# Pooled attention and a gated feed-forward layer: later key and value loads on another queue, key pooling at an earlier step

## The chip, the cores and the metric

The kernel runs on one core of a Trainium2 chip. The core has five engines that run their own instruction streams: PE (TensorE, matrix products into PSUM banks), DVE (VectorE, elementwise work), ACT (ScalarE, activations and copies), POOL (GpSimd) and SP (SyncE, which here only issues transfers). Transfers between the chip's memory (DRAM) and the core's on-chip memory are issued by an engine onto its queue and carried out by 16 DMA engines that all queues share. The metric is the device time of one execution, in microseconds (us), lower is better.

## What is computed

Attention over keys and values that are averaged in groups of 8, and then a feed-forward layer with a SiLU between its two products. Cut to its core:

```python
# q, k, v: (8 batches, 8 heads, 576 positions, 64); w_in: (512, 2048); w_out: (2048, 512)
k_p = k.reshape(B, H, Sp, 8, D).mean(axis=3)      # Sp = 72
v_p = v.reshape(B, H, Sp, 8, D).mean(axis=3)
scores = scale * np.matmul(q, k_p.transpose(0, 1, 3, 2))
attn = softmax(scores)
x = heads side by side of np.matmul(attn, v_p)    # (4608, 512)
h = x @ w_in
g = h * (1.0 / (1.0 + np.exp(-h)))
return g @ w_out                                  # (4608, 512)
```

## The kernel before

The 4608 tokens are worked through in nine blocks of 512, `t` = 0 to 8. Each block has two products. `up(t, ...)` multiplies by `w_in` and applies SiLU, giving `h_T`; `down(t, ...)` for block 0 and `down_quarters(t, ...)` for the others multiply by `w_out` and store the result. From block 1 on, the products save multiplications: a product is cut into quarters, sums of quarters are formed (on the left `x_sum` at L454 for the first product and `h_sum` at L614 for the second), and seven partial products, numbered 1 to 7, are made in place of eight.

`down_quarters` makes its seven partial products in the order 2, 5, 1, 4, 3, 7, 6, in 112 steps of one matmul each. They accumulate into three PSUM banks, `P` (2, 4, 7), `Q` (5, 3, 6) and `R` (1). Between them VectorE and ScalarE take intermediate results out of the banks: after partial product 3 a copy on VectorE takes `Q` out into `o_sb` (L681), after 7 an addition takes `P` out (L685), and after 6 an addition takes `Q` out again (L689). Partial product 6 accumulates onto `Q`, so its first matmul has to wait for the copy at L681.

The attention of batch `t + 1` runs inside block `t` as small pieces between the steps of the products. They are "fillers": pairs of a step number and a function, called by `spread` at that step, so that a filler's instructions stand on each engine's stream behind what was issued up to that step. The order of every engine's instructions is therefore written out by hand through these numbers; an instruction that waits holds up all that stand behind it on its engine.

The keys and values of batch 0 to 2 are loaded in another layout (`load_slots`). For batches 3 to 7 a tensor of one batch arrives in two halves: `load_one` loads the first four of each eight rows that are averaged (`PH` = 256 numbers for each of 72 groups and 8 heads) into the buffer `raw`, and `load_rest` (L182) loads the other four onto POOL's queue with an addition into the same place, so it waits until the first half has landed. `load_one` goes through `load_rows` (L173), which issues two transfers on SP's queue, of 64 and of 8 partitions. There is one buffer for the keys (`k_raw`) and one for the values (`v_raw`). The queries of the batch (`load_q`) go onto POOL's queue too.

SP's queue also carries the stores of `down_quarters`, 16 for a block (L566).

Pooling: `pool_k(b, 0)` adds halves of the loaded rows (L188), `pool_k(b, 1)` makes the last addition in two instructions into `kp` (L193), which `k_transpose` turns over in the next block. `pool_v` does the same for the values, at step 10 of the second product.

In block `t` from 1 to 5, with `a = t + 1`, the fillers are issued as follows: at step 0 of the first product the first half of the keys of batch `t + 2`; at step 1 its queries (in block 5 at step 48, as eight pieces); at step 2 the second half of the keys; in the second product at step 10 `pool_v` of batch `t + 1`, at step 11 the first half and at step 12 the second half of the values of batch `t + 2`; at step 100 both stages of `pool_k` of batch `t + 2`. Numerators of the attention (`xT`, L403) are filled in at steps 56, 97 and 101. The next block begins with the five `x_sum` instructions at step 0.

Of the kernel before, what the change touches and what calls it, by code (L numbers as in the profile page):

```python
# [36 lines left out]
def kernel(  # L37
# [9 lines left out]
    nc = tc.nc  # L47
# [3 lines left out]
    SP = S // POOL  # L51
# [107 lines left out]
    PH = POOL // 2 * D  # L159

    def raw_tile(tag, heads, full=False):
        raw = big.tile([128, H * PH], FP32, tag=tag, name="raw")
        if full:
            return raw
        return raw[:SP, : H * PH].rearrange("k (h e) -> k h e", h=heads)

    def source(b, name):
        return (k if name == "k" else v)[b].rearrange("h (sp p) d -> sp h (p d)", p=POOL)


    def load_rows(eng, out, in_):
        for r0, r1 in ((0, 64), (64, SP)):
            eng.dma_start(out=out[r0:r1], in_=in_[r0:r1])  # L173

    def load_one(b, name):
        st = batches.setdefault(b, {})
        raw = raw_tile(f"{name}_raw", H)
        load_rows(nc.sync, raw, source(b, name)[:, :, :PH])
        st[f"{name}_raw"] = raw

    def load_rest(b, name):
# [5 lines left out]
    def add_halves(raw):  # L187
        nc.vector.tensor_add(  # L188
            out=raw[:, :, : 2 * D], in0=raw[:, :, : 2 * D], in1=raw[:, :, 2 * D :]
        )  # L190

    def add_rest(dst, raw):
        nc.vector.tensor_add(  # L193
            out=dst,
            in0=raw[:, :, :D].rearrange("k h (c d) -> k h c d", c=2),
            in1=raw[:, :, D : 2 * D].rearrange("k h (c d) -> k h c d", c=2),
        )

    def pool_k(b, stage):
        st = batches[b]  # L200
        raw = st["k_raw"]
        if stage == 0:
            add_halves(raw)
            return
        for i in range(2):
            add_rest(
                kp[:SP, i].rearrange("k c s d -> k s c d"), raw[:, 4 * i : 4 * (i + 1)]
            )
# [7 lines left out]
    def k_transpose(b, parts=(0, 1)):  # L216
        st = batches[b]
        kT_ps = ps_tile([128, 2, 2, SP], FP32, "at", "kT_ps")
        for a in parts:
            for c in range(2):  # L220
                nc.tensor.matmul(
                    kT_ps[:, a, c, :],
                    lhsT=kp[:, a, c].rearrange("k s d -> k (s d)"),
                    rhs=ident[:, :SP], start=True, stop=True,
                )
        a0, a1 = parts[0], parts[-1] + 1
        nc.scalar.copy(kz[b % 2][:, a0:a1], kT_ps[:, a0:a1])
# [40 lines left out]
    def slot_sums(name, j, halves=False):  # L268
        raw = row_tiles[name][j]
        dst = rows5[name][:, SA:] if j else rows5[name][:, :SA]  # L270
        w = RE // 4 if halves else RE // 2
        while w > D:
            nc.vector.tensor_add(  # L273
                out=raw[..., :w], in0=raw[..., :w], in1=raw[..., w : 2 * w]
            )
            w //= 2
        nc.vector.tensor_add(out=dst, in0=raw[..., :D], in1=raw[..., D : 2 * D])
# [10 lines left out]
    def select_k(b, a):  # L288
        st = batches[b]
        if a == 0:  # L290
            st["kz_ps"] = ps_tile([128, 2, 2, SP], FP32, "at", "kz_ps")
        for c in range(2):
            for s in range(4):
                for i, r, sp, m in segments(4 * a + s):
                    nc.tensor.matmul(
                        st["kz_ps"][32 * s : 32 * (s + 1), a, c, sp : sp + m],
                        lhsT=k5[:, i, c * DH : (c + 1) * DH],
                        rhs=ident[:, r : r + m], start=True, stop=True,
                    )

    def copy_k(b, a, copy=nc.vector.tensor_copy):
        copy(out=kz[b % 2][:, a], in_=batches[b]["kz_ps"][:, a])

    def select_v(b, a, tag="at"):
        st = batches[b]
        if a == 0:
            st["v_ps"] = ps_tile([128, H, D], FP32, tag, "v_ps")
            st["vp"] = mid.tile([SP, H, D], BF16, tag="vp", name="vp")
        for h in range(4 * a, 4 * (a + 1)):
            segs = list(segments(h))  # L310
            for j, (i, r, sp, m) in enumerate(segs):
                x = SP + r - sp
                nc.tensor.matmul(
                    st["v_ps"][:, h, :], lhsT=shifts[:, x : x + 128], rhs=v5[:, i],
                    start=(j == 0), stop=(j == len(segs) - 1),
                )

    def copy_v(b, a, copy=nc.vector.tensor_copy):
        hs = slice(4 * a, 4 * (a + 1))
        copy(out=batches[b]["vp"][:, hs, :], in_=batches[b]["v_ps"][:SP, hs, :])  # L320
# [468 lines left out]
    for t in range(NT):  # L789
        a = t + 1  # L790
        f_up, f_down = [], []
# [40 lines left out]
        if a < B:  # L832
            q_at = [15, 16, 17, 8] if t > 1 else [24, 25, 26, 2] if t else [82, 84, 86, 88]
            if t == 0:
                for j in range(2):
                    f_up.append((44 + 8 * j, lambda j=j: slot_sums("k", j)))
                    f_up.append((72 + 8 * j, lambda j=j: select_k(1, j)))
                    f_up.append((72 + 8 * j, lambda j=j: copy_k(1, j)))
                    f_down.append((20 + 10 * j, lambda j=j: slot_sums("v", j)))
                    f_down.append((37 + 3 * j, lambda j=j: select_v(1, j, "at")))  # L840
                    f_down.append((37 + 3 * j, lambda j=j: copy_v(1, j)))
            elif t == 1:
                for j in range(2):
                    f_up.append((0, lambda j=j: slot_sums("k", j, halves=True)))
                    f_up.append((22, lambda j=j: select_k(2, j)))
                    f_up.append((23, lambda j=j: copy_k(2, j)))
                    f_down.append((8, lambda j=j: slot_sums("v", j, halves=True)))
                    f_down.append((40, lambda j=j: select_v(2, j, "at")))
                    f_down.append((41, lambda j=j: copy_v(2, j)))
            else:  # L850
                f_up.append((22, lambda: k_transpose(a)))
                f_down.append((10, lambda: pool_v(a)))
            for n in range(4):
                f_to = f_down if t and n == 3 else f_up
                f_to.append((q_at[n], lambda n=n: q_transpose(a, n % 2, n // 2)))
            if t == 0:
                f_down.append((0, lambda: load_half_2("k", 0)))
                f_down.append((0, lambda: load_q(2)))
                f_down.append((0, lambda: load_half_2("k", 1)))
                for half in range(2):  # L860
                    f_down.append((31, lambda half=half: load_half_2("v", half)))
                for y in range(2):
                    for n in U_W:
                        f_down.append((6, lambda y=y, n=n: unit_weight_sum(y, n)))
            elif a + 1 < B:
                for stage in range(2):
                    f_down.append((100, lambda stage=stage: pool_k(a + 1, stage)))
                f_up.append((0, lambda: load_one(a + 1, "k")))
                f_up.append((48 if a + 1 == B - 1 else 1, lambda: load_q(a + 1)))
                f_up.append((2, lambda: load_rest(a + 1, "k")))  # L870
                f_down.append((11, lambda: load_one(a + 1, "v")))
                f_down.append((12, lambda: load_rest(a + 1, "v")))
            f_down.append((0, attn_tables))

            if t:
                sc_at, den_at, nu_at = (1, 31, 75), (31, 56, 97), (56, 97, 101)
            else:
                sc_at, den_at, nu_at = (1, 16, 30), (16, 30, 44), (44, 55, 56)
            for n, sg in enumerate(visits):
                f_down.append((den_at[n], lambda sg=sg: denominators(a, sg)))  # L880
                f_down.append((sc_at[n], lambda sg=sg: scores(a, sg)))

            for n, sg in enumerate(visits):
                if n < 2 or not 0 < t < B - 2:
                    f_down.append((nu_at[n], lambda sg=sg: numerators(a, sg)))
                if n == 0 and 1 < t < B - 1:
                    f_down.append((nu_at[n], lambda: numerators(a - 1, visits[2])))
# [34 lines left out]
```

The softmax here doesn't subtract the row's maximum and nothing guards it: scores larger than these inputs give would overflow.

## Time and profile before

| what | value |
|---|---|
| runs of this kernel | median 286.65 us (285.92, 286.42, 286.87, 287.04) |
| the profiled execution | 286.42 us, span 284.5 us |
| queue of POOL (software_dynamic) | 20.86 MB, 45.0% of the 16 DMA engines' span |
| queue of SP (hardware_dynamic) | 15.48 MB, 22.9% |
| SP issues of first halves (L173) | 20, median 0.60 us each, 57.2 to 191.3 us |
| POOL issues of second halves (L182) | 10, 1.38 to 1.43 us each |
| L182, issue to landing | 8.4, median 8.9, at most 11.3 us |
| L188 on VectorE | 10, median 1.195 us |
| L193 on VectorE into `kp` | 10, median 0.418 us |

The span runs from the first to the last instruction of the profiled execution; its time has what lies around it too. A group of a profile's rows gives a line of the kernel, an engine, the operation with output and input, the number of instructions, the busy time and the idle time of the engine just before. "Landing" is the time from the issue of a transfer until its data is in place. In a timeline a row's idle time and what ended it stand in square brackets. The chain of waits is followed back from the last instruction to what released each step, and is printed in order of time.

### The profile page before, as it was taken

To read this page: it belongs to the slowest core of one execution; us is meant where nothing else is said; L and a number is where in the kernel's file an instruction comes from. 1 tells how busy PE (TensorE), PEld (TensorE's weight loads), DVE (VectorE), ACT (ScalarE), POOL (GpSimd) and SP (SyncE) were. 2 spreads that over 40 slices of the span, in tenths; PEclk is the share of its full clock that TensorE was granted. 3 is DMA by queue.
4 is the path that set the end of the run, shared out by engine and by line. 5 is a ranking of instruction groups with operands and counts; after the bars stand their busy time and mean duration, and the time that the engine had idled before them with its cause. 6 is when DMAs were issued, how large, how long until landed. Compare 5 with 4: busy or idle time off the path is not lost.

```text
span 284.5 us, 6941 instructions
## 1 busy us (share of the span) xinstructions
PE 277.8 (98%) x2793; PEld 194.2 (68%) x2793; DVE 225.2 (79%) x404; ACT 183.7 (65%) x359; POOL 52.1 (18%) x68
## 2 busy tenths in 40 slices
PE   8989999999999999999999999999999999999995
PEld 3338544556777777667888785687667767787684
DVE  4986837899789896979697959886998686836773
ACT  1678765667577866687668856794779567325700
POOL 8744317312030013001020101062100000000000
PEclk9999999999999999999999999999999999999999
DMA  7999999894949557964979386739970032005004
GB/s 212 277 267 227 216 311 163 213 193 88 153 76 200 135 98 117 180 174 65 129 130 225 61 142 121 180 51 159 146 138 0 2 97 53 2 9 140 1 4 147
DMA packets 35296, 37.70 MB, mean 133 GB/s; under 512 B 9952, under 2 KB 27616, under 8 KB 35264
## 3 DMA queue, kind: packets, MB, share of 16 engines
q0 software_dynamic: 21760, 20.86, 45.0%
q1 hardware_dynamic: 12928, 15.48, 22.9%
q10 hardware_dynamic: 576, 0.92, 0.9%
q8 instruction: 22, 0.36, 0.6%
q14 instruction: 10, 0.08, 0.1%
HBM read 36.70 MB, written 9.44 MB: 162 GB/s over the span
## 4 chain that ended last, share of the span: by engine, by line
PE 87%; DVE 5%; DMA 3%; issue 1%; ACT 1%; SPq 1%; DVEq 0%; POOLq 0%
PE hp_ps L546 24%; PE o_psP L654 15%; PE o_psQ L654 14%; PE u_psQ L487 7%; PE u_psP L487 7%; PE o_psR L654 5%; PE sc_ps L350 4%; PE o_ps L581 3%; PE u_psR L487 2%; PE nu_ps L394 2%; DMA q_bf<-in_q_dram 2%; PE den_ps L368 2%; DMA out_dram<-o_sb 1%; SPq L566 1%; DVE w_sum L632 1%
## 5 line engine op out<-in xcount | busy, mean ns | idle before, releaser
L546 PE MATMUL hp_ps<-xT,w_in_sb 128*128 128x512 bf16 (+3 forms) x412 | 82.6, 340 | 0.5 <-ACT h_T L552 0.4
L552 ACT ACTIVATE h_T<-hp_ps 128x512 bf16<-128x512 f32 (+2 forms) x95 | 51.3, 545 | 26.9 <-PE hp_ps L546 25.6
L654 PEld LDWEIGHTS <-h_sum 128*128 128x128 bf16 x640 | 60.6, 98 | 12.0 <-issue 1.3
L546 PEld LDWEIGHTS <-w_in_sb 128*128 128x128 bf16 x412 | 39.3, 98 | 25.0 <-issue 1.4
L614 DVE TENSOR_TENSOR h_sum<-h_T 128x1024 bf16<-128x1024 bf16 (+1 forms) x72 | 50.8, 743 | 6.9 <-ACT h_T L552 6.9
L358 ACT ACTIVATE es<-sc_ps 72x384 bf16<-72x384 f32 (+1 forms) x100 | 38.9, 468 | 9.8 <-PE sc_ps L350 9.7
L487 PEld LDWEIGHTS <-w_sum 128*128 128x128 bf16 x300 | 29.2, 98 | 9.2 <-DVE x_sum L454 1.6
L654 PEld LDWEIGHTS <-h_T 128*128 128x128 bf16 x256 | 24.1, 98 | 4.4 <-issue 0.9
L403 DVE TENSOR_TENSOR xT<-nu_ps,rec 128x384 bf16<-128x384 f32 (+1 forms) x50 | 24.0, 532 | 0.3
L377 ACT ACTIVATE lnd<-den_ps 128x384 f32<-128x384 f32 (+1 forms) x23 | 11.1, 483 | 19.8 <-PE den_ps L368 19.8
L153 DVE STREAM_TRANSPOSE qT<-q_bf 128x576 bf16<-128x576 bf16 x32 | 23.0, 754 | 0.0
L495 ACT ACTIVATE h_T<-c_sb 128x512 bf16<-128x512 f32 x30 | 18.1, 625 | 5.0 <-DVE c_sb L519 5.0
L182 POOL DMA_DIRECT2D raw<-in_k_dram x5 | 7.0, 1397 | 74.2 <-DVE h_sum L614 24.0
L273 DVE TENSOR_TENSOR raw<-raw 128x384 f32<-128x384 f32 (+3 forms) x20 | 12.3, 614 | 8.3 <-DMA raw<-in_v_dram 4.7
L654 PE MATMUL o_psP<-w_out_sb,h_sum 128*128 128x256 bf16 x128 | 17.6, 273 | 0.0
L654 PE MATMUL o_psQ<-w_sum,h_sum 128*128 128x256 bf16 x128 | 16.7, 273 | 0.0
L654 PE MATMUL o_psQ<-w_out_sb,h_sum 128*128 128x256 bf16 x128 | 16.6, 273 | 0.0
L654 PE MATMUL o_psQ<-w_sum,h_T 128*128 128x256 bf16 x128 | 16.5, 273 | 0.0
L654 PE MATMUL o_psP<-w_sum,h_T 128*128 128x256 bf16 x128 | 16.5, 273 | 0.0
L654 PE MATMUL o_psR<-w_sum,h_sum 128*128 128x256 bf16 x128 | 15.7, 273 | 0.0
L182 POOL DMA_DIRECT2D raw<-in_v_dram x5 | 6.9, 1390 | 47.4 <-DVE kp L193 11.6
L654 PE MATMUL o_psP<-w_sum,h_sum 128*128 128x256 bf16 x128 | 15.4, 272 | 0.0
(78 smaller groups left out, 417.6 us busy)
## 6 DMA issues: line engine op xcount, KB each, us to landing
out_dram<-o_sb SPq DMA_DIRECT2D x128, 64.0 KB, 3.2
q_bf<-in_q_dram POOLq DMA_DIRECT2D x6, 576.0 KB, 11.7
raw<-in_k_dram SPq DMA_DIRECT2D x6, 512.0 KB, 5.3
raw<-in_k_dram POOLq DMA_DIRECT2D x5, 576.0 KB, 9.9
raw<-in_v_dram POOLq DMA_DIRECT2D x5, 576.0 KB, 8.7
raw<-in_v_dram SPq DMA_DIRECT2D x5, 512.0 KB, 9.6
w_in_sb<-in_moe_w_in_dram POOLq DMA_DIRECT2D x8, 256.0 KB, 8.6
w_out_sb<-in_moe_w_out_dram POOLq DMA_DIRECT2D x4, 512.0 KB, 13.6
```

The lines of the kernel that those rows point to most:

```text
L153: nc.vector.transpose(out=st["qT"][:, a, f * QF : (f + 1) * QF].rearrange("r i c p -> r (i c p)"), in_=st["q_bf"][:, a, f * n : (f + 1) * n],)
L182: nc.gpsimd.dma_start(out=batches[b][f"{name}_raw"], in_=source(b, name)[:, :, PH:], accum_op=ALU.add,)
L273: nc.vector.tensor_add(out=raw[..., :w], in0=raw[..., :w], in1=raw[..., w : 2 * w])
L350: nc.tensor.matmul(sc[s][:, cs], lhsT=kz[b % 2][rows, g, c, :], rhs=st["qT"][rows, g, i0:i1, c, :], start=(c == 0), stop=(c == 1),)
L358: nc.scalar.activation(es[:, s, :], sc[s], func=AF.Exp, scale=score_scale)
L403: nc.vector.tensor_mul(out=xT[:, 2 * g0 + c : 2 * (g0 + ng - 1) + c + 1 : 2, cols], in0=nu[c][:, :w].rearrange("r (g n) -> r g n", g=ng), ...
L487: nc.tensor.matmul(ps[bank][:, u, :], lhsT=w[:, kk, 128 * u : 128 * (u + 1)], rhs=x[:, kk, :], start=first and u == 0 and kk == 0, stop=kk ...
L495: nc.scalar.activation(h_T[:, g : g + 2, j * NQ : (j + 1) * NQ], src, func=AF.Silu)
L546: nc.tensor.matmul(hp_ps[:, r0:r1], lhsT=w_in_sb[:, kk, g * 128 : (g + 1) * 128], rhs=xT[:, kk, x0 : x0 + r1 - r0], start=(kk == 0), stop= ...
L552: nc.scalar.activation(h_T[:, g, n0 : n0 + n], hp_ps[:, :n], func=AF.Silu)
L614: nc.vector.tensor_tensor(out=h_sum[n][:, ks, :], in0=quarter(*a, ks), in1=quarter(*b, ks), op=op)
L654: nc.tensor.matmul(ps[b][:, c, :], lhsT=left(n, kt, c), rhs=W_OUT[n][:, kt, :], start=b not in begun, stop=kt == k1 - 1, skip_group_check= ...
```

## The change

The first halves of keys and values of batches 3 to 7 are issued on POOL's queue, as one transfer of 72 partitions, in place of two on SP's. The two stages of `pool_k` are issued at steps 73 and 81 of the second product in place of both at step 100. The step numbers of the loads are unchanged. In POOL's stream this gives, for each block from 1 to 5: first half of keys, queries, second half of keys, first half of values, second half of values.

```diff
-    def load_rows(eng, out, in_):
-        for r0, r1 in ((0, 64), (64, SP)):
-            eng.dma_start(out=out[r0:r1], in_=in_[r0:r1])
-
     def load_one(b, name):
         st = batches.setdefault(b, {})
         raw = raw_tile(f"{name}_raw", H)
-        load_rows(nc.sync, raw, source(b, name)[:, :, :PH])
+        nc.gpsimd.dma_start(out=raw, in_=source(b, name)[:, :, :PH])
         st[f"{name}_raw"] = raw
...
             elif a + 1 < B:
                 for stage in range(2):
-                    f_down.append((100, lambda stage=stage: pool_k(a + 1, stage)))
+                    f_down.append((73 + 8 * stage, lambda stage=stage: pool_k(a + 1, stage)))
                 f_up.append((0, lambda: load_one(a + 1, "k")))
                 f_up.append((48 if a + 1 == B - 1 else 1, lambda: load_q(a + 1)))
                 f_up.append((2, lambda: load_rest(a + 1, "k")))
                 f_down.append((11, lambda: load_one(a + 1, "v")))
                 f_down.append((12, lambda: load_rest(a + 1, "v")))
```

## The prediction, made before the changed kernel was run

> **What bounds the kernel now.** The page comes first: who is busy.
>
> ```profile
> span 284.5 us, 6941 instructions
> PE 277.8 (98%) x2793; PEld 194.2 (68%) x2793; DVE 225.2 (79%) x404; ACT 183.7 (65%) x359; POOL 52.1 (18%) x68
> PEclk9999999999999999999999999999999999999999
> raw<-in_k_dram SPq DMA_DIRECT2D x6, 512.0 KB, 5.3
> raw<-in_k_dram POOLq DMA_DIRECT2D x5, 576.0 KB, 9.9
> raw<-in_v_dram POOLq DMA_DIRECT2D x5, 576.0 KB, 8.7
> ```
>
> TensorE is busy for 98% of the span at full clock, so the moves of this change can only win back the few gaps in it, or make new ones. Next comes the list of who waited for whom, for the gaps that touch the moved work.
>
> ```profile
> DVE raw L188 <- DMA raw<-in_k_dram: 1.6, 2, 1.0
> PE u_psR L487 <- DVE x_sum L454: 1.0, 2, 0.7
> ```
>
> Twice VectorE waits for keys (1.6 us in all), twice TensorE waits for `x_sum`. The chain of waits shows where: a block's second product begins at these pieces (blocks 2 to 6).
>
> ```profile
> 95.77 0.22 PE o_psP L654 x2
> 125.55 0.22 PE o_psP L654 x2
> 154.72 0.22 PE o_psP L654 x2
> 184.85 0.22 PE o_psP L654 x2
> 213.95 0.22 PE o_psP L654 x2
> ```
>
> I call such a start D. The periods are 29.78, 29.17, 30.13 and 29.10 us. Blocks 2 and 4 hold the two waits; block 5, without one, is the clean period. Their excess over it is 0.68 and 1.03 us, close to the waits of 0.64 and 0.99 us in VectorE's timeline. That timeline, end of block 2's second product:
>
> ```profile
> 105.83 0.68 DVE L614 TENSOR_TENSOR h_sum<-h_T 128x1024 bf16<-128x1024 bf16 x1
> 107.55 0.69 DVE L681 COPY o_sb<-o_psQ 128x512 f32<-128x512 f32 x1 [1.04 <-PE o_psQ L654]
> 109.35 0.69 DVE L685 TENSOR_TENSOR o_sb<-o_psP,t_sb 128x512 f32<-128x512 f32 x1 [1.11 <-PE o_psP L654]
> 109.97 1.02 DVE L403 TENSOR_TENSOR xT<-nu_ps,rec 128x384 bf16<-128x384 f32 x2
> 111.63 1.22 DVE L188 TENSOR_TENSOR raw<-raw 72x1024 f32<-72x1024 f32 x1 [0.64 <-DMA raw<-in_k_dram]
> 112.89 0.76 DVE L193 TENSOR_TENSOR kp<-raw 72x256 bf16<-72x256 f32 x2
> 113.56 0.68 DVE L689 TENSOR_TENSOR o_sb<-o_psQ,t_sb 128x512 f32<-128x512 f32 x1
> ```
>
> The key pooling (L188, L193) stands between `xT` and L689 with the five `x_sum` behind it; ahead of L681 and L685 VectorE idles 1.04 and 1.11 us. Why the keys are late is in the queues' timelines:
>
> ```profile
> 80.97 13.54 SPq L566 DMA_DIRECT2D out_dram<-o_sb  x16
> 94.61 1.17 SPq L173 DMA_DIRECT2D raw<-in_k_dram  x2
> 101.12 1.39 POOL L182 DMA_DIRECT2D raw<-in_k_dram  x1 [18.12 <-DVE raw L188]
> 110.27 1.40 POOL L182 DMA_DIRECT2D raw<-in_v_dram  x1 [7.77 <-DVE o_sb L685]
> 111.09 1.33 POOL L145 DMA_DIRECT2D q_bf<-in_q_dram  x1
> ```
>
> The key buffer was free at 83.8 (end of block 1's L193), but the load stood behind 16 stores on SP until 94.61. The second half, which adds onto the first, left when that had landed, and landed just before 111.63.
>
> **The change, part by part.**
>
> *Issues.* SP loses 20 load issues of about 0.6 us (the L173 rows' median); its stores wait on VectorE's results, so 0 on the path. POOL gains 10 issues. Nearest row: L182, same 72 rows, 1.39 us; 10 x 1.39 = 13.9 us on an engine busy 52.1 of 284.5, with 75.5 us idle before its last store. Worth 0, unless POOL's order delays a transfer, which comes next.
>
> *The chain of loads.* One POOL queue now issues, per block: first half of v, second half of v (waits for the first to land), first half of the next k, q, second half of that k (waits again). No row shows a first half on POOL. Bounds from the L182 rows (second halves, same shape and queue): 8.4, median 8.9, at most 11.3 us from issue to landing; below by the fastest SP row, 4.8 us, which would only bring keys earlier and gain no more. I take the median of L182, the nearest row. So:
> - the v buffer is free at D + 5.8 (in block 2 SP issued v at 101.6); landed + 8.9 (8.4 to 11.3) = D + 14.7;
> - v's second half leaves, k's first 0.8 later (110.27 to 111.09, where q stands now), queued behind it beside the stores as q is today, which landed 11.6 to 12.8 us after issue, median 11.7: D + 27.2;
> - k's second half + 8.9 (8.4 to 11.3): D + 36.1. Less the clean period of 29.1, that is the next block's D + 7.0; lowest rows D + 5.9, highest D + 13.0.
>
> *The pooling's new place.* The built program puts L188 between the L614 and L681 above and the two L193 between L681 and L685. VectorE is ready at 106.5 = D + 10.7. L188 takes 1.25 to the next start, so L681 begins at 107.76, 0.2 late, and ends at 108.45. The product that accumulates onto the bank it reads begins at 109.09: hidden by 0.6 us. The L193 pair (0.68) runs from 108.4 to 109.1, before L685 at 109.35, unmoved. So 1.93 us (111.63 to 113.56) leave the stretch ahead of `x_sum`, and go into 2.15 us of idle time. In the clean blocks TensorE waits for nothing there, so they gain 0. In blocks 2 and 4 the waits of 0.64 and 0.99 go, if keys land by D + 10.7 + 0.6 = D + 11.3. Behind a late L188 now stand L681, and so the last product itself: past D + 11.3 each microsecond is one of TensorE's. By the median rows there are 4.3 us to spare.
>
> *First and last batch.* Block 1: k's first half takes q's slot at 56.4 + 0.8, landing as q did there in 10.6: 67.8; second half + 8.9 = 76.7, against VectorE ready at 76.87 and TensorE's limit near 78.1 (80.16 less L681's 0.69, L188's 1.25 and 0.1): just in time, at 11.3 it costs 1.0. Block 5: the last q, in eight pieces, moves up with k's second half (187.4 before), the last v queues behind them. They were all in by 202.7; even with no gain v would land by 202.7 + 2 x 8.4 = 219.5 against a use at 217.9, a 1.6 us delay of VectorE early in a product; with q issued some 5 us earlier, in time. I take 0 for both.
>
> *A rule against it.* Trace row: in blocks 2 to 5 a first half of k took 4.8 to 6.2 us on SP. The Trainium skill, "DMA: Bandwidth & Descriptors", section "Issuing engine by pattern", gives plain loads to SyncE and calls its path generally the faster; section "Issuing engines are not separate DMA queues" says another issuer saves only issue time. By these the queue's change would bring nothing and the sum stay at 286.4. What the trace sets against them is the 10.8 us (83.8 to 94.61) that the load stood behind stores.
>
> *Sum.* 0.68 + 1.03 = 1.7 us off. The profiled execution took 286.4 us (span 284.5), so 284.7; the median of the runs, 286.65, is 0.2 above it: **284.9 us**.
>
> **The rivals.**
>
> 1. *Keys late at their new place (slower).* Place: L188 ahead of L681. With the highest rows in every step they land at D + 13.0, 1.7 past the limit. It limits itself: a stall of 1.7 moves the next D by as much, while v's load was issued before the stall, so the next batch is in time. Blocks 2 and 4 stall, 1.0 in block 1: 2 x 1.7 + 1.0 - 1.7 = +2.7, 289.4 us. It decides from a landing of D + 11.3 on and is slower than the noise when stalls pass 2.6 us. If first halves took 1 us more than the highest row, that adds 2 us to each of the two stalls: 293.4. For: five dependent transfers in one queue, and k's second half took 10.5 and 11.3 in blocks 2 and 4. Against: in both, SP's load of v ran beside it, which now queues behind. Chance 0.28.
>
> 2. *The wait is hidden anyway (no change).* The chain of waits names a store's landing, not the keys, in those two gaps. If stores or stray timing make them, pooling elsewhere brings at most a part: 286.4. Against: VectorE's idle time in front of L188 (0.64, 0.99) equals the periods' excess (0.68, 1.03). Chance 0.10.
>
> 3. *VectorE becomes the bound in the middle (slower by little).* If L188 and L193 overfill the 2.15 us, L681 frees the bank late: the 0.6 us of cover must first go in each of five blocks; with 1 us over, 5 x 0.4 - 1.7 = +0.3, 286.9, within noise. Chance 0.04.
>
> **How the numbers follow.** Forecast 0.58, rivals 0.28, 0.10 and 0.04. 0.3% of 286.65 is 0.86 us, about what a measurement can tell from no change. Faster by more (below 285.8): 0.58. Within: rivals 2 and 3 less a little, plus the mildest of rival 1: 0.14. Slower: 0.28. The likeliest case alone spans 284.0 (runs went down to 285.9, less 1.7, rounded) to 285.7. The range takes in rival 1 with the highest rows (289.4) and a little more, 284.0 to 290.0; left out are rival 1 beyond those rows, some 0.1, and 0.05 below.
>
> **What would show it.** Right: no idle time before L188 for a key transfer; the POOL queue issuing k's first half right behind v's second, near D + 15; D to D of 29.1 to 29.2 in blocks 2 to 5; no TensorE wait on `x_sum`; L681 some 0.2 us later after D. Wrong: L188 idle on `in_k_dram` between L614 and L681, TensorE waiting at the last product (L654, bank Q) for L681, periods above 30; or landings of first halves on POOL well above 11 us. A period that stays near 30 with no wait at L188 would leave the cause of the two gaps elsewhere.

## The result and the profile after

| kernel | median (lowest to highest) | runs |
|---|---|---|
| before | 286.34 us (285.25 to 287.47) | 72 |
| changed | 285.45 us (284.81 to 286.33) | 46 |

The ratio is 0.9968, with a 95% interval of 0.9961 to 0.9976: 0.9 us less, between 0.69 and 1.12. The forecast of 284.9 us had the right sign and gave about twice the gain. The profiled execution took 285.56 us.

The page of the changed kernel, its span and engines, then its two main queues (packets, megabytes, share of the 16 DMA engines' span), then two groups of DMA issues (count, size of one, median time from issue to landing):

```profile
span 283.7 us, 6909 instructions
PE 277.7 (98%) x2793; PEld 194.4 (69%) x2793; DVE 225.7 (80%) x404; ACT 183.5 (65%) x359; POOL 60.6 (21%) x78
q0 software_dynamic: 23840, 26.77, 52.3%
q1 hardware_dynamic: 6928, 9.58, 12.3%
raw<-in_k_dram POOLq DMA_DIRECT2D x10, 576.0 KB, 9.6
raw<-in_v_dram POOLq DMA_DIRECT2D x10, 576.0 KB, 7.8
```

5.9 MB have gone from SP's queue to POOL's, and POOL has ten more instructions. TensorE has the same work. The starts of the second products, which the prediction calls D, in the chain of waits (start, duration):

```profile
96.25 0.22 PE o_psP L649 x2
...
125.35 0.22 PE o_psP L649 x2
...
154.52 0.22 PE o_psP L649 x2
...
183.70 0.22 PE o_psP L649 x2
...
212.79 0.22 PE o_psP L649 x2
```

The periods are now 29.10, 29.17, 29.18 and 29.09 us: all four are like the clean ones, and TensorE's waits for `x_sum` are gone from the list of waits. Lines of the changed kernel are five lower than before's (before's L188 is now L183, its L193 is now L188). VectorE's timeline, end of block 2's second product:

```profile
106.31 0.68 DVE L609 TENSOR_TENSOR h_sum<-h_T 128x1024 bf16<-128x1024 bf16 x1
106.91 1.22 DVE L183 TENSOR_TENSOR raw<-raw 72x1024 f32<-72x1024 f32 x1
108.05 0.68 DVE L676 COPY o_sb<-o_psQ 128x512 f32<-128x512 f32 x1
108.65 0.75 DVE L188 TENSOR_TENSOR kp<-raw 72x256 bf16<-72x256 f32 x2
109.85 0.69 DVE L680 TENSOR_TENSOR o_sb<-o_psP,t_sb 128x512 f32<-128x512 f32 x1 [0.45 <-PE o_psP L649]
110.46 1.02 DVE L398 TENSOR_TENSOR xT<-nu_ps,rec 128x384 bf16<-128x384 f32 x2
112.24 0.69 DVE L684 TENSOR_TENSOR o_sb<-o_psQ,t_sb 128x512 f32<-128x512 f32 x1 [0.76 <-PE o_psQ L649]
112.84 1.76 DVE L449 TENSOR_TENSOR x_sum<-xT 128x512 bf16<-128x512 bf16 x5
```

The pooling fills the idle time ahead of L676 and more than half of that ahead of L680 (0.45 us of 1.11 are left), without any wait of its own. The copy at L676 starts at D + 11.80; before it was D + 11.78. And the keys' loads, POOL's timeline around the same place (`issue` in brackets means that the profile shows nothing that ended the idle time):

```profile
102.37 0.84 POOL L173 DMA_DIRECT2D raw<-in_v_dram  x1 [8.10 <-DVE vp L188]
109.10 1.40 POOL L177 DMA_DIRECT2D raw<-in_v_dram  x1 [5.90 <-issue]
109.94 1.40 POOL L173 DMA_DIRECT2D raw<-in_k_dram  x1
110.76 1.32 POOL L145 DMA_DIRECT2D q_bf<-in_q_dram  x1
122.71 1.43 POOL L177 DMA_DIRECT2D raw<-in_k_dram  x1 [10.63 <-DMA raw<-in_k_dram]
```

This is the chain of five transfers, in the order forecast. Keys leave at D + 13.7 behind the values and not at the next block's start behind stores; the second half leaves 2.6 us ahead of the next D. SP's queue carries only stores from here on. In block 5 the order differs: the queries, in eight pieces, go out behind the keys' second half (from 181.26).

### The profile page after: what moved, and what is told of

Its sections match the earlier page's. It is cut to its first block, busy times and chain, and to the rows that moved or that the text cites. A ratio compares the mean times of both kernels' runs of the same rounds, so it can differ in the third digit from the quotient of the medians.

```text
span 283.7 us, 6909 instructions
## 1 busy us (share of the span) xinstructions
PE 277.7 (98%) x2793; PEld 194.4 (69%) x2793; DVE 225.7 (80%) x404; ACT 183.5 (65%) x359; POOL 60.6 (21%) x78
## 4 chain that ended last, share of the span: by engine, by line
PE 80%; DMA 15%; DVE 2%; POOL 1%; issue 1%; POOLq 0%
PE hp_ps L541 21%; PE o_psP L649 15%; PE o_psQ L649 15%; PE u_psP L482 7%; PE u_psQ L482 7%; PE o_psR L649 5%; DMA w_out_sb<-in_moe_w_out_dram 5%; DMA q_bf<-in_q_dram 4%; DMA raw<-in_k_dram 4%; PE sc_ps L345 3%; DMA raw<-in_v_dram 3%; PE u_psR L482 2%; PE nu_ps L389 2%; PE den_ps L363 2%; DVE w_sum L627 1%
## 5 line engine op out<-in xcount | busy, mean ns | idle before, releaser
L553 POOL DMA_DIRECT2D out_dram<-o_sb x1 | 0.6, 615 | 79.6 <-issue 79.6
L514 DVE TENSOR_TENSOR c_sb<-u_psP,t_sb 128x512 f32<-128x512 f32 x15 | 10.3, 689 | 8.2 <-PE u_psP L482 3.6
## 6 DMA issues: line engine op xcount, KB each, us to landing
w_out_sb<-in_moe_w_out_dram POOLq DMA_DIRECT2D x4, 512.0 KB, 13.7
raw<-in_v_dram POOLq DMA_DIRECT2D x2, 768.0 KB, 11.4
raw<-in_k_dram POOLq DMA_DIRECT2D x1, 768.0 KB, 10.1
```

What stands on the lines that cost most here:

```text
L514: tt(out=c_sb[0], in0=ps["P"], in1=t_sb, op=ALU.add)
```

## The experiments

The theory, A: the keys' first half stood behind a block's 16 stores on SP, so that its second half landed after VectorE was ready for it; on POOL it stands behind nothing late. Rivals: B, the new place of the pooling makes the gain, by freeing the stretch ahead of `x_sum`; C, the values' first half on SP slowed the keys' second half, which ran beside it, and moving the values makes the gain; and rival 2 of the prediction, the gain has nothing to do with the keys' wait.

### The queue alone, and the place alone

The changed kernel with the pooling put back at step 100 (the same line stands in both edits, in opposite directions):

```diff
-                    f_down.append((73 + 8 * stage, lambda stage=stage: pool_k(a + 1, stage)))
+                    f_down.append((100, lambda stage=stage: pool_k(a + 1, stage)))
```

> First halves on POOL, key pooling left at step 100. Theory A (the gain is keys that land sooner because their first half no longer stands behind 16 stores on SP): second half of k issued near D - 3, landed near D + 7, ahead of L183 at D + 15, no wait on keys; all periods from D to D of blocks 2 to 5 at 29.1 to 29.2 us; ratio as the whole change, 0.997 (0.996 to 0.998). Theory B (the gain is the 1.93 us of VectorE work taken off the stretch ahead of x_sum): periods of blocks 2 and 4 stay above 29.5, ratio 1.000.

Measured: 285.46 us, ratio 0.997 (0.9957 to 0.9983), no wait of the pooling for keys, and from the first D to the sixth 146.21 us, as in the changed kernel (212.79 - 66.58). So the queue makes the whole gain, and B falls: the place adds nothing that can be measured.

The kernel before with the pooling at steps 73 and 81:

```diff
-                    f_down.append((100, lambda stage=stage: pool_k(a + 1, stage)))
+                    f_down.append((73 + 8 * stage, lambda stage=stage: pool_k(a + 1, stage)))
```

> First halves on SP as before, key pooling at steps 73 and 81. Theory A: k lands at D + 14 to D + 16 in blocks 2 to 5 but is wanted at D + 11.3, and the store wait that makes it late moves along with the stall, so each of four blocks loses 3 to 4.6 us, block 1 little: 297 to 304 us, ratio 1.04 to 1.065, L188 idle on in_k_dram and TensorE waiting for L681. Theory B: as the whole change or better, 0.997.

Measured: 298.42 us, ratio 1.0424 (1.0403 to 1.0444). The total is as expected, its distribution isn't: blocks 2 and 4 stall, the others hardly. Its lists of waits (total, times, longest):

```profile
DVE raw L188 <- DMA raw<-in_k_dram: 11.7, 3, 5.5
PE o_psQ L654 <- DVE o_sb L681: 9.1, 2, 4.7
```

Where it happens in block 2, in VectorE's and then TensorE's timeline:

```profile
112.30 1.22 DVE L188 TENSOR_TENSOR raw<-raw 72x1024 f32<-72x1024 f32 x1 [5.53 <-DMA raw<-in_k_dram]
113.44 0.68 DVE L681 COPY o_sb<-o_psQ 128x512 f32<-128x512 f32 x1
...
107.60 1.91 PE L654 MATMUL o_psP<-w_sum,h_sum 128*128 128x256 bf16 x16
114.17 0.59 PE L654 MATMUL o_psQ<-w_sum,h_sum 128*128 128x256 bf16 x2 [4.66 <-DVE o_sb L681]
```

VectorE waits 5.53 us for keys at the pooling; the copy out of bank Q stands behind it; the last product needs the bank. So the cover is 0.87 us (5.53 less 4.66) before TensorE stands still. SP's timeline shows why block 3 gets off lightly:

```profile
101.87 1.17 SPq L173 DMA_DIRECT2D raw<-in_v_dram  x2
115.42 12.84 SPq L566 DMA_DIRECT2D out_dram<-o_sb  x16
128.36 1.17 SPq L173 DMA_DIRECT2D raw<-in_k_dram  x2
```

Block 3 has its D at 131.97. The stores of block 2 begin when VectorE has taken results out, and after the stall the block still takes its time, so the keys leave 3.6 us ahead of D in place of 1.6 us in block 2 (94.40 against 96.02). Block 3 then waits 0.91 us, of which its period shows 0.2 (29.37 against 29.17), and block 4 stalls again by 5.29.

The two periods with stalls are 35.95 and 35.30 us, 6.85 and 6.12 over the changed kernel's (29.10 and 29.18). That is more than TensorE's idle 4.66 and 4.42. The profile's windows over the first stall show the rest (columns: stretch, length, busy time and count of PE, PEld, DVE, ACT, POOL, then the granted clock, DMA share, GB/s):

```profile
110.00:111.00 1.00, 0.00 (x0) 0.00 (x0) 0.00 (x0) 0.00 (x0) 0.00 (x0) 1.00 0.44 82
111.00:112.00 1.00, 0.00 (x0) 0.00 (x0) 0.00 (x0) 0.00 (x0) 0.00 (x0) 0.87 0.07 12
112.00:114.00 2.00, 0.00 (x0) 0.00 (x0) 1.70 (x2) 0.00 (x0) 0.71 (x1) 0.50 0.00 0
114.00:116.00 2.00, 1.83 (x24) 0.88 (x24) 1.81 (x5) 0.64 (x2) 1.44 (x2) 0.50 0.24 22
116.00:118.00 2.00, 2.00 (x11) 1.44 (x10) 0.60 (x2) 1.66 (x2) 0.00 (x0) 0.50 0.97 119
118.00:119.00 1.00, 1.00 (x7) 0.65 (x6) 0.14 (x1) 0.00 (x0) 0.00 (x0) 0.72 1.09 150
119.00:121.00 2.00, 1.95 (x13) 1.15 (x12) 2.00 (x6) 1.02 (x2) 0.00 (x0) 1.00 1.14 178
```

TensorE stood still from 109.51; the granted clock halves inside the gap and comes back at about 118.56 (a mean of 0.72 in the slice from 118 is half speed for 0.56 of it). From 114.17 on, 4.4 us at half speed lose 2.2, and 4.66 + 2.2 is the 6.85.

In the second stall the clock falls at another moment. TensorE's row, then the windows:

```profile
179.25 0.38 PE L654 MATMUL o_psQ<-w_sum,h_sum 128*128 128x256 bf16 x2 [4.42 <-DVE o_sb L681]
...
179.00:180.00 1.00, 0.75 (x22) 0.48 (x21) 1.00 (x4) 0.00 (x0) 0.63 (x1) 1.00 0.00 0
180.00:181.00 1.00, 1.00 (x16) 0.56 (x7) 1.00 (x3) 0.93 (x2) 0.00 (x0) 0.50 0.42 57
...
183.00:184.00 1.00, 0.89 (x6) 0.53 (x5) 0.53 (x1) 0.00 (x0) 0.00 (x0) 0.79 0.91 137
```

Here the clock halves at 180.00, when TensorE has been at work again for 0.75 us, and comes back at about 183.42 (0.79 is half speed for 0.42 of the slice). 3.4 us at half speed lose 1.7, and 4.42 + 1.7 is the 6.12.

### Keys alone, and values alone

The kernel before with one tensor's first halves on POOL (for the second kernel the test is for "v"):

```diff
-        load_rows(nc.sync, raw, source(b, name)[:, :, :PH])
+        if name == "k":
+            nc.gpsimd.dma_start(out=raw, in_=source(b, name)[:, :, :PH])
+        else:
+            load_rows(nc.sync, raw, source(b, name)[:, :, :PH])
```

> The kernel before with the first halves of the keys alone on POOL; values on SP, pooling at step 100. Theory A (stores on SP hold back k's first half): the queue of the keys is all that counts; k's second half issued at D - 3 or sooner, no wait at L188, periods 29.1 to 29.2, ratio 0.997. Theory C (k is late because its second half moves beside SP's first half of v): the same ratio, as the early k meets no v.

> The kernel before with the first halves of the values alone on POOL; keys on SP behind the stores, pooling at step 100. Theory A: k's second half still leaves at D + 5.3 and lands at D + 15.5 to 16.5, so the waits at L188 stay (0.6 to 1.2 us in some blocks), ratio 1.000. Theory C: v now moves behind k's second half in one queue, which lands in 8.4 to 8.9 us instead of 9.9 to 11.3, at D + 14.2, ahead of L188 at D + 15.2: no wait, periods 29.1 to 29.2, ratio 0.997. Either way v's second half leaves later than in the whole change.

Measured: keys alone 285.13 us, 0.9955 (0.9939 to 0.9971), no wait for keys, 146.14 us from the first D to the sixth. Values alone 286.06 us, 0.999 (0.9976 to 1.0004), with one wait of 0.20 us and 146.43. Both were run again:

> Keys alone on POOL, pooling at step 100, timed again beside the changed kernel. If values on POOL add nothing: the same as e11 within 0.15%. If moving the values costs something: 0.1% faster than e11, as the first two timings hint (0.9955 and 0.9976).

> Values alone on POOL, a second profile, as the first had one wait of 0.20 us at L191 while its time was only 0.1% below before. Theory A: waits at L191 of 0.3 to 1.2 us in all, smaller and rarer than before's 0.74 to 1.96, since k's second half still leaves at D + 5.3 and lands within half a microsecond of its use. Theory C: none.

Measured: keys alone 285.28 us, 0.9971 (0.9952 to 0.9989), again 146.14 and no wait; values alone, one execution of 286.08 us, one wait of 0.56 and 146.81. So the keys' move suffices, which is A. The first run of values alone met neither expectation: its one wait is shorter than A's 0.6 to 1.2, and C had none; the second's 0.56 is within A's 0.3 to 1.2. C looks to hold in part: with the values moved the waits of two executions (0.20 and 0.56) are below those of the kernel before, seen below, and the keys' second half landed after 8.0 to 10.1 us in blocks 2 to 4, against 9.3 to 11.4 in three profiles of the kernel before. Two executions don't tell how large that part is.

Moving the values as well wins nothing once the keys are moved. The times, 285.28 us with the keys alone and 285.47 for the changed kernel on the same chip, don't tell the two apart, but the profiles put the changed kernel some 0.3 us behind: 0.07 from the first D to the sixth (146.14 against 146.21), 0.13 in the closing waits (below), and 0.10 between the sixth D and the end of the last VectorE instruction. That last stretch is 67.68 or 67.69 us in seven profiles with the values on SP and 67.77 to 67.79 in seven with them on POOL; why is not shown.

### On SP's queue, but ahead of the stores

This tells the queue from the place in it. The kernel before with the early pooling that cost 4.2%, and its keys still on SP, but issued at step 90 of the block before, when the pooling has freed the buffer and no store of that block has been issued:

```diff
-                    f_down.append((100, lambda stage=stage: pool_k(a + 1, stage)))
-                f_up.append((0, lambda: load_one(a + 1, "k")))
+                    f_down.append((73 + 8 * stage, lambda stage=stage: pool_k(a + 1, stage)))
+                if t == 1:
+                    f_up.append((0, lambda: load_one(a + 1, "k")))
+                if a + 2 < B:
+                    f_down.append((90, lambda: load_one(a + 2, "k")))
```

> Everything on SP's queue as before, but the first half of the next keys issued at step 90 of the second product, ahead of that block's 16 stores in SP's stream, with key pooling at steps 73 and 81. Theory A (place in the queue behind the stores, not the queue itself): the load leaves at about D + 14, the second half near D + 20, landed by D + 32 of the same block, which is D + 3 of the next, so the early pooling costs nothing: no wait at L188, periods 29.1 to 29.2 us, ratio 0.996 to 0.997, although the same steps 73 and 81 gave 1.042 with the load behind the stores. Rival (SP's path itself is too slow for the early place): stalls at L188, ratio above 1.01.

Measured: 285.04 us, 0.9968 (0.9949 to 0.9987), no wait for keys, 146.14 us from the first D to the sixth. SP's and POOL's timelines in block 2:

```profile
109.43 1.17 SPq L173 DMA_DIRECT2D raw<-in_k_dram  x2
110.69 14.88 SPq L566 DMA_DIRECT2D out_dram<-o_sb  x16
...
119.06 1.40 POOL L182 DMA_DIRECT2D raw<-in_k_dram  x1 [7.93 <-DVE qT L153]
```

The keys leave at 109.43, ahead of the stores, and their second half at 119.06, 3.7 us earlier than in the changed kernel. Same queue and same early pooling as the kernel of 298.42 us: the place in SP's stream alone takes the ratio from 1.0424 to 0.9968. Rival 2 falls too, since the stores are all there and the two gaps are gone.

### The same kernels again: how much is there to win?

If the two waits that vanish cost 1.7 us in one execution, why is the gain 0.9? The two kernels were profiled again.

> The changed kernel once more. Both theories: 0.997. A second profile: if the changed kernel's periods are steady, D of block 6 less D of block 1 is 146.2 us again (it was 146.21), and what differs between executions lies ahead of block 1 and behind block 6.

> The changed kernel on the same chip as e9 and e10, for comparison: 0.997, D of block 6 less D of block 1 of 146.2 us.

> The kernel before once more, for a second profile. If my sum of 1.7 us came from an execution with unusually late keys, D of block 6 less D of block 1 is here nearer 147.1 than 147.85, with waits at L188 of about 0.9 us in all in place of 1.63. If the measured gain is smaller because the changed kernel loses time elsewhere, it is 147.8 again.

> The kernel before a third time, for a third profile of the waits at L188: 1.63 and 1.96 us so far, in blocks 2 and 4 and in blocks 2 and 3. If the measured gain of 0.9 is what waits of this size give less what the changed kernel loses at its end, D of block 6 less D of block 1 is 147.5 to 148.3 again; if the first two were unusual, nearer 147.1.

Measured, changed kernel: 285.47 us, 0.9976 (0.9963 to 0.9988), and 285.47 us, 0.9982 (0.9966 to 0.9999); both 146.22 us from the first D to the sixth, no wait for keys. The kernel before:

| profile of before | waits at L188 | first D to sixth | less 146.21 |
|---|---|---|---|
| first (286.42 us) | 0.64 + 0.99 = 1.63 | 147.85 | 1.64 |
| second (286.94 us) | 0.77 + 1.19 = 1.96 | 148.15 | 1.94 |
| third (286.17 us) | 0.74 | 146.95 | 0.74 |

In each execution the excess is the wait to 0.02 us; but how much it waits, and in which blocks, differs: in blocks 2 to 4 the keys' second half leaves 3.4 to 5.9 us behind D and takes 9.3 to 11.4 us to land. The mean of the three is 1.44.

### The last 0.25 us

Behind the last VectorE instruction the changed kernel needed 3.08 us to the end of its span in three profiles, and the kernel before 2.83 (the expectation below has both from spans rounded to 0.1 us). A completion semaphore is a counter that a transfer raises when it has landed. Eight of them go round in turn, and at the program's end SP waits for each in a fixed order: the closing checks. With 20 transfers fewer on SP, the last store is given another of the eight. To test it, one store of block 3 in the changed kernel was cut in pieces, four more transfers on SP, so that the last store gets the semaphore that it has in the kernel before:

```diff
-            engines[u % len(engines)].dma_start(
-                out=rows[:, cs], in_=src[QP * u : QP * (u + 1)]
-            )
+            step = QP // 2 if (t, m) == (3, 0) else QP
+            for r in range(0, QP, step):
+                engines[u % len(engines)].dma_start(
+                    out=rows[r : r + step, cs],
+                    in_=src[QP * u + r : QP * u + r + step],
+                )
```

> The changed kernel with one 128-token store of block 3 cut into pieces of 16 rows, four transfers more on SP, so that the last store has the completion semaphore that it has in the kernel before. If the 0.25 us that the changed kernel loses behind its last VectorE instruction (3.08 to 3.13 us to the end of the span, 2.87 before) come from the place of that semaphore in the closing checks, it is 2.87 again and the time 0.25 lower than the changed kernel's: ratio 0.996. If not, 3.1 and 0.997.

Measured: 2.83 us in this profile; 146.22 us from the first D to the sixth; 285.39 us, 0.9959 (0.9943 to 0.9975). The profile shows the 0.25 us; the times don't tell the two kernels apart. SP's closing wait for the stores (total, times, longest) in the changed kernel:

```profile
SPq L912 <- DMA out_dram<-o_sb: 1.3, 1, 1.3
```

and with the pieces:

```profile
SPq L915 <- DMA out_dram<-o_sb: 1.0, 2, 0.8
```

One wait of 1.3 us, after which every check that comes later in the list is still to be made, becomes two, of at most 0.8, with checks between them. In the traces the last store has the fifth semaphore of the order in the kernel before and with the pieces, and the first in the changed kernel, so four more checks come behind its landing; they start 0.06 us apart, and four make the 0.25 us. The kernels with one tensor moved, 10 transfers fewer on SP, have the third and lie in the middle: 2.94 to 2.95 us in four profiles.

## Why the prediction was right, and where it was off

**The cause** was right. The keys' first half stood behind stores on SP, and taking it out from behind them removes the waits: by POOL's queue (0.9955 and 0.9971 with the keys alone) or by an earlier place on SP (0.9968).

**The chain of loads** was right in its order and close in its times. The values' first half landed after 5.5 to 6.1 us and not the 8.9 taken from second halves: in block 2 the values' second half left at D + 12.9 where D + 14.7 was forecast. The keys' first half followed 0.84 us later there, as forecast (1.25 to 2.2 in the other blocks), and took 11.5 to 12.6 us to land beside the queries (forecast 11.6 to 12.8). The keys' second half left at the next D less 2.6 us (forecast 1.9) and landed after 7.5 to 9.6. In blocks 2 to 5 the keys were in place at D + 4.8 to 6.3 (forecast 7.0), ahead of VectorE, which is ready at D + 10.7. The two ends cost nothing, as forecast: block 1's keys were in place at 73.99, used at 77.28, and the last values at 207.15, used at 217.06.

**The pooling's new place** was put at a gain of 0, and that held. The copy behind it was forecast 0.2 us late and came 0.02 late. The `x_sum` group starts at D + 16.59, with nothing won by it once the keys are in time.

**The size** was off in one term: "0.68 + 1.03 = 1.7 us off". The two waits of one execution were taken as those of every execution. They add to 1.63, 1.96 and 0.74 us in three, a mean of 1.44. (The other 0.07 of the 1.7 is lost again in the changed kernel: its block 4 takes 29.18 us and not the clean 29.10, which the kernels with the keys alone keep.) What else was not foreseen: 0.25 us in the closing checks, on the other side, and 0.10 between the sixth D and the last VectorE instruction (67.78 us to its end in three profiles of the changed kernel, 67.68 in three of the kernel before), which goes with the values' move. 1.44 - 0.25 - 0.10 is 1.1, at the upper end of the measured 0.69 to 1.12. Three executions are few; what makes these moments and landings differ from one to the next stays open. The spread of all runs fits it, without proving it: 2.2 us before (285.25 to 287.47) and 1.5 after.

**Rival 1** is real, but not in this kernel. The early pooling with late keys costs 12 us. Its place (L188 ahead of the copy), its alternation (blocks 2 and 4, there because the stores run ahead of a late D) and its cover (0.6 forecast, 0.87 measured) are seen there; its price of one TensorE microsecond for each one late is too low, as the clock adds 1.7 to 2.2 us to a stall (6.12 for 4.42, 6.85 for 4.66).

**Rival 2** (stores, not keys, make the two gaps) is refuted by the kernels in which all stores remain on SP and the waits are gone. **Rival 3** would need a late copy; 0.02 us isn't one.

**The rule weighed against the change.** In the runs the queue as such makes no difference that can be measured: keys on POOL 285.13 and 285.28 us, keys on SP ahead of the stores 285.04. The Trainium skill, "DMA: Bandwidth & Descriptors", section "Issuing engines are not separate DMA queues", says that transfers run on the same 16 DMA engines whichever engine starts them; nothing here speaks against that. It also says that another issuer saves only issue time, and the sum of 286.4 us worked out from that was not what was measured: what was saved is the 10.8 us that the load stood behind stores on its issuer.

## What to carry to other kernels

A load that waits for nothing may still be late because of the stores in front of it on its engine: look at when its buffer came free and when it left, and if the two are far apart, move it ahead of the stores or to another issuer; either does. Move only the load that is late; the values' move won nothing here. Such a move comes first and the early use second: the same pooling place costs 4.2% without it and nothing with it. Before a wait is priced, it should be seen in more than one execution; here it was 0.74 to 1.96 us in the same kernel.

## What the runs showed of the hardware that was not expected

Two gaps of 4.66 and 4.42 us at TensorE cost 6.85 and 6.12 us. In the first the granted clock fell to 0.50 some 2.2 us into the gap and stayed there for 4.4 us of work after it; in the second it fell 5.2 us after the last product, with TensorE at work again, and stayed for 3.4 us. In the trace the clock's changes around the two, at 111.74, 118.56, 180.00 and 183.42 us, stand 2, 18 and 1 times 3.413 us apart, and in the changed kernel its first rise and last fall (6.06 and 282.54) 81 times. So here it changes on a beat, and the price of a gap hangs on where the beat falls and not on the gap's length alone. The gaps of 0.3 to 0.9 us in three profiles of the kernel before left it at full speed; no run has one between 0.9 and 4.4. The Trainium skill, "TensorE: Matmul & The Clock Gate", section "Why this matters for your kernels", asks for no idle gaps of TensorE above some 3 us for this reason; the two gaps, both longer, agree, and the limit itself is not measured here.

The second thing is the 0.25 us at the program's end, which followed from the number of transfers issued on SP before it: 2.83 us behind the last VectorE instruction with all of them, 2.95 with 10 fewer, 3.08 with 20 fewer, and 2.83 again with 16 fewer, two full rounds of the eight semaphores.
